# The last block of w2 in two transfers, of 119 rows and of 9 rows

## The chip, the cores and the metric

The kernel runs on one core of one Trainium2 chip. The metric is the device time of one execution in microseconds (us), taken as the median of several executions. The engines are named as in the profile: PE is TensorE, DVE is VectorE, ACT is ScalarE, POOL is GpSimd, SP is SyncE. SP issues nearly all transfers here; "SPq" in the profile is SP's issuing of them.

## What is computed

One decode step of a transformer layer: attention against a cache of 4,096 keys, and then a feed-forward block with the mish activation. Both have a layer norm ahead of them and a residual sum behind. In the reference, cut to what matters:

```python
# A: B=4, Sq=1, D=640, H=32, Sk=4096, Dh=128 (all bf16)
def A(x, k_cache, v_cache, wq, wo):
    q = (x @ wq).reshape(B, Sq, H, Dh).transpose(0, 2, 1, 3)
    scores = einsum("bhqd,bhkd->bhqk", q, k_cache) * Dh ** -0.5
    o = einsum("bhqk,bhkd->bhqd", softmax(scores), v_cache)
    return o.transpose(0, 2, 1, 3).reshape(B, Sq, H * Dh) @ wo

# B: F=1728
def Bff(x, w1, b1, w2):
    h = einsum("bsd,df->bsf", x, w1) + b1
    sp = log1p(exp(-abs(h))) + where(h > 0, h, 0)
    return einsum("bsf,fd->bsd", h * tanh(sp), w2)

h  = x + A(layernorm(x), k_cache, v_cache, wq, wo)
out = h + Bff(layernorm(h), w1, b1, w2)
```

The two caches are 268 MB together; w2 is a matrix of 1,728 rows of 640 numbers, 1,280 B a row.

## The kernel before

The cache is worked through in 16 units, each of eight heads of one batch element. A unit has 8 MB of K and 8 MB of V. Three large buffers of SBUF (`slot`) take turns: while one unit's K is multiplied by the query on DVE (line 614) and summed on PE with an identity matrix (line 626), the next V and K are on their way. The softmax goes over DVE, PE and ACT (lines 663 to 717), the product with V over PE (line 736).

The order of all work is written out by hand. `Program.add` records each operation with the names that it reads and writes; `Program.plan` works out which operation has to wait for which, and `Program.emit` writes the instructions engine by engine, in the order of recording. A transfer raises a semaphore by 16 when it has landed. Where two transfers are given the same semaphore, the counts add up, and who needs both waits once, for the sum.

SP's transfers stand in one queue in the order of recording. Behind the last part of V come, all through the helper `load` (its transfer is line 854): four transfers of wo, five of w1, the 64 remaining rows of w2 (line 873), and then w2 in pieces that get smaller towards the end. The pieces are given by `W2P = (0, 6, 10, 12, C2)` with C2 = 13: blocks 0 to 5, 6 to 9, 10 and 11, and block 12 alone. A block is 128 rows, one row for each partition of SBUF. In the first three pieces a partition takes pairs of neighbouring rows, so each run in memory is 2,560 B; block 12 is odd and has runs of one row, 1,280 B. It is the last transfer into the core.

What reads them stands at the end of the program. Line 941 projects the attention's output by wo; line 901 (`tt`, the helper for sums and products on DVE) adds the residual; lines 978 to 1030 are the second layer norm, with the matmuls by w1 (line 1003) between them; lines 1034 to 1062 the activation. Then PE multiplies by w2 (line 1070): first the remaining 64 rows, then piece by piece, each piece after a wait for its own transfer, named `("w2", k0)`. Five matmuls belong to a block. The sum of all is added to the residual on DVE (line 901), turned by one matmul (line 1087), copied (line 1094), and stored by SP (line 1095) as 20 rows of 256 B.

Of the kernel before, what the change touches and what calls it, by code (L numbers as in the profile page):

```python
# [223 lines left out]
def kernel(  # L224
# [15 lines left out]
    B, Sq, D = A_x.shape  # L240
# [49 lines left out]
    S_BANK, TR, QQ, OB, OT = [("bank", i) for i in range(4)], *[("bank", i) for i in range(4, 8)]  # L290
# [45 lines left out]
    def cells(i, lo=0, hi=SLOT):  # L336

        return [("slot", i, p, k) for p in range(lo // PART, -(-hi // PART)) for k in range(NQ)]
# [470 lines left out]
    def slot_of(u):  # L809
        return 1 if u == 0 else 2 * u % NS  # L810
# [21 lines left out]
    i1, i2, i3 = slot_of(NU - 1), slot_of(NU - 2), slot_of(NU - 3)  # L832
# [7 lines left out]
    w2_sb = wend2[:, 0 : C2 * D].rearrange("p (k n) -> p k n", k=C2)  # L840
    w2r_sb = wend2[:, C2 * D : nw2]
    C2E = C2 - C2 % 2
    w2_view = B_w2[0 : C2E * 128, :].rearrange("(m p k) n -> p m (k n)", p=128, k=2)

    def load(out_ap, in_ap, i, lo, hi, name, sem=None):


        ops = {}
        for cell in cells(i, lo, hi):
            for d in P.readers.get(cell, {}).values():  # L850
                ops[d.nth] = d
        P.add(
            "SP",
            lambda: nc.sync.dma_start(out=out_ap, in_=in_ap),  # L854
            w=[name],
            sem=sem or "_".join(map(str, name)),
            after=ops.values(),
        )
# [18 lines left out]
    for k0, k1 in zip(W2P, W2P[1:]):  # L877
        if k0 < C2E:
            assert k0 % 2 == k1 % 2 == 0
            to = wend2[:, k0 * D : k1 * D].rearrange("p (m n) -> p m n", n=2 * D)  # L880
            of = w2_view[:, k0 // 2 : k1 // 2]
        else:
            to, of = w2_sb[:, k0, :], B_w2[k0 * 128 : k1 * 128, :]
        load(to, of, i2, k0 * D, k1 * D, ("w2", k0))

    at = [nw2]

    def scratch(n, dt=FP32):
        a = at[0]
        w = n * (2 if dt == FP32 else 1)  # L890
        w += w % 2
        at[0] = a + w
        ap = wend2[:, a : a + w]
        return ap.bitcast(FP32)[:, 0:n] if dt == FP32 else ap[:, 0:n]

    def do(eng, emit, r=(), w=()):

        return P.add(eng, emit, r=r, w=w, after=[last_pv])
# [167 lines left out]
    def w2_products(blocks):  # L1066
        for c in blocks:
            w2 = w2_sb[:, c, :] if c < C2 else w2r_sb
            for dc in range(DC):
                ins = nc.tensor.matmul(  # L1070
                    y2T[:, dc, :],
                    lhsT=w2[:, dc * 128 : (dc + 1) * 128],
                    rhs=act_t[:, c, :],
                    start=(c == C2 and dc == 0),
                    stop=(c == C2 - 1 and dc == DC - 1),
                )
        return ins

    do("PE", lambda: w2_products([C2]), ["w2r", "act"], [S_BANK[1]])
    for k0, k1 in zip(W2P, W2P[1:]):  # L1080
        do("PE", lambda b=range(k0, k1): w2_products(b), [("w2", k0), "act"], [S_BANK[1]])
    oT = scratch(N * DC, BF16).rearrange("p (n c) -> p n c", n=N)
    tt(oT.rearrange("p n c -> p c n"), hT, y2T, ALU.add, ["hT", S_BANK[1]], ["oT"])
    o_ps = tr_bank[0 : N * DC, 0:128]
# [45 lines left out]
```

## Time and profile before

| | us |
|---|---|
| median of 3 runs | 667.02 |
| lowest and highest of them | 666.62, 667.08 |
| the profiled execution, its own time | 667.18 |
| its span, first to last instruction | 665.4 |
| busy: PE, DVE, ACT | 378.6, 353.6, 88.5 |
| traffic | 283.52 MB, 426 GB/s in the mean |

The transfers of the end, as the profile lists them by line, form and size, with the median from issue to landing:

| transfer | count | KB each | us to landing |
|---|---|---|---|
| wo | 4 | 1280 | 33.2 |
| w1 | 5 | 432 | 29.7 |
| w2, the remaining 64 rows | 1 | 80 | 20.7 |
| w2, blocks 0 to 5 | 1 | 960 | 20.3 |
| w2, blocks 6 to 9 | 1 | 640 | 19.2 |
| w2, blocks 10 and 11 | 1 | 320 | 13.4 |
| w2, block 12 | 1 | 160 | 12.0 |

A view of the profile counts time from the start of the span. In the chain of waits a line has its start, its length, and the engine and line that the time belongs to. In the DMA view "GB/s" is a row of 40 numbers, one for each fortieth of the window, and "packets" counts the pieces that the 16 DMA engines moved: a piece is one run of a transfer (here a row of w2, or a pair of rows), or a record of 4 B with which an engine reports that its share of a transfer is done.

### The profile page before, as it was taken

What the parts mean: (1) busy time and instruction counts of PE and PEld (TensorE: products, weight loads), DVE (VectorE), ACT (ScalarE), POOL (GpSimd) and SP (SyncE); (2) the same over time, 40 slices, a digit from 0 to 9 for tenths busy, and PEclk for the clock granted to TensorE, in tenths of its full rate; (3) what the DMA queues carried; (4) which work ended last, traced back from release to release, by engine and by line L of the source; (5) the groups of instructions that cost most, each with busy time, mean ns of one, the idle gap of its engine ahead of it and who ended that gap; (6) DMA issues with size and microseconds to landing.
All of it is one profiled execution on the core that took longest, in us unless ns stands there. A gap on an engine that the chain in (4) does not pass through costs nothing.

```text
span 665.4 us, 6915 instructions
## 1 busy us (share of the span) xinstructions
PE 378.6 (57%) x2804; PEld 173.4 (26%) x2804; DVE 353.6 (53%) x315; ACT 88.5 (13%) x316; POOL 2.4 (0%) x12
## 2 busy tenths in 40 slices
PE   0354778375482837558283755828375582827764
PEld 0221333132230313223031322303132230313343
DVE  2075869083573809357380845738084573818501
ACT  0102020202002020200202020020202002020211
POOL 1000000000000000000000000000000000000000
PEclk9999799788596978869697796969779695977965
DMA  9999999999999999999999999999999999999996
GB/s 379 438 441 438 437 415 418 438 437 430 441 437 433 433 418 437 437 429 441 433 437 433 418 437 437 429 441 429 441 433 418 437 437 429 437 433 418 420 415 247
DMA packets 7571, 283.52 MB, mean 426 GB/s; under 512 B 835, under 2 KB 1031, under 8 KB 2440
## 3 DMA queue, kind: packets, MB, share of 16 engines
q1 hardware_dynamic: 7550, 283.35, 99.0%
q8 instruction: 8, 0.13, 0.1%
q14 instruction: 3, 0.02, 0.0%
q10 hardware_dynamic: 10, 0.01, 0.0%
HBM read 283.35 MB, written 0.01 MB: 426 GB/s over the span
## 4 chain that ended last, share of the span: by engine, by line
DMA 43%; DVE 25%; PE 21%; another core or an unknown queue 6%; issue 2%; SPq 1%; ACT 1%; DVEq 0%; ACTq 0%
DMA slot<-in_A_k_cache_dram 41%; DVE slot L614 21%; PE bank L626 13%; PE bank L736 6%; DVE s_sb L601 3%; DMA slot<-in_B_w_dram 2%; SPq L854 1%; ACT e L711 1%; PE bank L694 0%; DVE slot L901 0%; PE bank L769 0%; DVE mx L681 0%; DVE rl L788 0%; PE bank L672 0%
## 5 line engine op out<-in xcount | busy, mean ns | idle before, releaser
L626 PE MATMUL bank<-slot,ident 128*128 128x512 bf16 x1024 | 272.6, 421 | 245.8 <-DVE slot L614 245.8
L614 DVE TENSOR_TENSOR slot<-slot,qb 128x4096 bf16<-128x4096 bf16 x128 | 288.3, 2284 | 156.1 <-DMA slot<-in_A_k_cache_dram 151.6
L626 PEld LDWEIGHTS bank<-slot,ident 128*128 128x128 bf16 x1024 | 101.0, 106 | 402.6 <-DVE slot L614 278.2
L601 DVE TENSOR_REDUCE s_sb<-bank 128x64 f32<-128x512 f32 x64 | 44.0, 688 | 57.3 <-PE bank L626 57.3
L711 ACT ACTIVATE e<-s_sb,nb 128x256 bf16<-128x256 f32 x128 | 63.1, 494 | 46.6 <-DVE nb L703 46.6
L736 PE MATMUL bank<-slot,e 128*32 128x512 bf16 x1024 | 60.9, 392 | 0.0
L581 ACT CAST qb<-bank 128x128 bf16<-128x128 f32 x17 | 4.5, 266 | 307.7 <-PE bank L572 307.7
L736 PEld LDWEIGHTS bank<-slot,e 128*32 128x32 bf16 x1024 | 26.2, 99 | 33.2 <-issue 9.0
L756 ACT COPY o_sb<-bank 128x512 f32<-128x512 f32 x16 | 9.4, 586 | 180.3 <-PE bank L736 180.3
L681 DVE TENSOR_REDUCE mx<-bank 1x8 f32<-1x128 f32 x16 | 4.5, 278 | 39.9 <-PE bank L672 39.9
L711 ACT ACTIVATION_READ_ACCUMULATOR e<-s_sb,nb 128x1 f32 x128 | 23.9, 186 | 0.0
L769 PE MATMUL bank<-sel,o_sb 128*128 128x8 f32 x136 | 17.6, 256 | 0.0
L769 PEld LDWEIGHTS bank<-sel,o_sb 128*128 128x128 f32 x136 | 16.6, 192 | 0.0
L521 PE MATMUL bank<-xT,slot 128*128 128x4 bf16 x160 | 4.4, 168 | 10.7 <-DMA slot<-in_A_wq_dram 10.7
L694 PE MATMUL bank<-mx,nscale 1*128 1x8 f32 x32 | 6.1, 262 | 5.9 <-DVE mx L681 5.9
L788 DVE RECIPROCAL rl<-bank 128x8 f32<-128x8 f32 x17 | 3.4, 201 | 9.1 <-PE bank L769 9.1
L555 DVE COPY b1T<-bank 128x14 f32<-128x14 f32 x1 | 0.2, 173 | 14.0 <-PE bank L545 14.0
L694 PEld LDWEIGHTS bank<-mx,nscale 1*128 1x128 f32 x32 | 4.7, 182 | 10.6 <-DVE mx L681 10.6
L941 PE MATMUL bank<-slot,slot 128*128 128x4 bf16 x160 | 4.9, 166 | 4.4 <-DMA slot<-in_A_wo_dram 4.4
L767 PEld LDWEIGHTS bank<-rs,ones_f 128*128 128x128 f32 x34 | 6.3, 190 | 3.4 <-ACT o_sb L756 1.2
L521 PEld LDWEIGHTS bank<-xT,slot 128*128 128x128 bf16 x160 | 4.3, 104 | 10.8 <-DMA slot<-in_A_wq_dram 10.8
L663 DVE TENSOR_REDUCE pm<-s_sb 128x1 f32<-128x256 f32 x16 | 6.7, 420 | 0.5
(74 smaller groups left out, 70.5 us busy)
## 6 DMA issues: line engine op xcount, KB each, us to landing
slot<-in_A_v_cache_dram SPq DMA_DIRECT2D x4, 2048.0 KB, 42.8
slot<-in_A_wq_dram SPq DMA_DIRECT2D x1, 5120.0 KB, 15.2
slot<-in_A_wo_dram SPq DMA_DIRECT2D x4, 1280.0 KB, 33.2
slot<-in_B_w_dram SPq DMA_DIRECT2D x5, 432.0 KB, 29.7
slot<-in_B_w_dram SPq DMA_DIRECT2D x1, 960.0 KB, 20.3
slot<-in_B_w_dram SPq DMA_DIRECT2D x1, 640.0 KB, 19.2
slot<-in_B_w_dram SPq DMA_DIRECT2D x1, 320.0 KB, 13.4
slot<-in_A_k_cache_dram SPq DMA_DIRECT2D x16, 49.9
```

The source lines that it names most:

```text
L521: ins = nc.tensor.matmul(qT_ps[:, :, h], lhsT=wq_sb[:, c, h * Dh : (h + 1) * Dh], rhs=xT[:, c, :], start=(c == 0), stop=(c == DC - 1),)
L601: lambda: nc.vector.tensor_reduce(out=s_sb[:, part * RP : (part + 1) * RP], in_=s_bank[part][:, :].rearrange("p (r w) -> p r w", w=W), axi ...
L614: return nc.vector.tensor_tensor(out=kt, in0=kt, in1=qbs[u % NS][:, k * DQ : (k + 1) * DQ] .unsqueeze(1) .to_broadcast([128, RP, DQ]), op= ...
L626: ins = nc.tensor.matmul(s_bank[part][:, :].rearrange("p (r w) -> p r w", w=W), lhsT=ident[:, :], rhs=kt[:, :, d : d + W], start=(d == 0), ...
L663: lambda: nc.vector.tensor_reduce(out=pm[:, :], in_=s_sb[:, :], axis=AX.X, op=ALU.max),
L694: lambda: nc.tensor.matmul(nb_ps, lhsT=nscale[:, :], rhs=mx[:, :], start=True, stop=True),
L711: ins = nc.scalar.activation(out=e2[:, :, h, :], in_=s_sb[:, :].rearrange("p (g r) -> p g r", r=RQ), func=ACT.Exp, bias=nb[:, h : h + 1], ...
L736: ins = nc.tensor.matmul(o_bank[t : t + G * RQ, :], lhsT=e2[:, g, :, :], rhs=vt[:, g * RQ : (g + 1) * RQ, :], start=(g < CT), stop=(g >= N ...
L756: lambda: nc.scalar.copy(out=o_sb[:, :], in_=o_bank[:, :]),
L767: nc.tensor.matmul(l_ps, lhsT=ones_f[:, :], rhs=rss[u % NS][:, :], start=True, stop=True)
L769: ins = nc.tensor.matmul(o_ps, lhsT=o_sb[:, r * Dh : (r + 1) * Dh], rhs=sel[:, r, :], start=(r == 0), stop=(r == RQ - 1),)
L854: lambda: nc.sync.dma_start(out=out_ap, in_=in_ap),
```

## The change

Block 12 of w2 comes by two transfers: its first 119 rows, and behind them its last 9 rows. Both are issued by `load` at line 854, one after the other, and raise the same semaphore; the matmuls of block 12 wait for the sum of both. What is read, where it is put and what is computed from it stay the same.

```diff
         if k0 < C2E:
             assert k0 % 2 == k1 % 2 == 0
             to = wend2[:, k0 * D : k1 * D].rearrange("p (m n) -> p m n", n=2 * D)
             of = w2_view[:, k0 // 2 : k1 // 2]
+            load(to, of, i2, k0 * D, k1 * D, ("w2", k0))
         else:
-            to, of = w2_sb[:, k0, :], B_w2[k0 * 128 : k1 * 128, :]
-        load(to, of, i2, k0 * D, k1 * D, ("w2", k0))
+
+            for part, p in enumerate((slice(0, 119), slice(119, 128))):
+                load(
+                    w2_sb[p, k0, :],
+                    B_w2[k0 * 128 + p.start : k0 * 128 + p.stop, :],
+                    i2,
+                    k0 * D,
+                    k1 * D,
+                    ("w2", k0, part),
+                    f"w2_{k0}",
+                )
...
     for k0, k1 in zip(W2P, W2P[1:]):
-        do("PE", lambda b=range(k0, k1): w2_products(b), [("w2", k0), "act"], [S_BANK[1]])
+        names = [("w2", k0)] if k0 < C2E else [("w2", k0, part) for part in range(2)]
+        do("PE", lambda b=range(k0, k1): w2_products(b), [*names, "act"], [S_BANK[1]])
```

## The prediction

> **What bounds the kernel now.** I read the page first: the chain that ended last and the DMA row over the span.
>
> ```profile
> DMA  9999999999999999999999999999999999999996
> ...
> DMA 43%; DVE 25%; PE 21%; another core or an unknown queue 6%; issue 2%; SPq 1%; ACT 1%; DVEq 0%; ACTq 0%
> ```
>
> The 16 DMA engines are busy from end to end; only the last of 40 slices (16.6 us each) shows a 6. The kernel is a stream of 283 MB, and the change touches its last 160 KB, so only the tail counts. I therefore read the chain in order of time over the last 36 us, and SP's timeline beside it:
>
> ```profile
> 640.88 6.68 SPq L854
> 647.57 0.04 issue
> 647.61 13.37 DMA slot<-in_B_w_dram
> 660.98 0.05 issue
> 661.02 0.72 PE bank L1070 x15
> 661.74 0.02 issue
> 661.77 0.23 DVE slot L901
> ```
> ```profile
> 647.61 1.78 SPq L854 DMA_DIRECT2D slot<-in_B_w_dram  x1
> 649.43 0.89 SPq L854 DMA_DIRECT2D slot<-in_B_w_dram  x1
> ```
>
> The first of the two issues is blocks 10 and 11 of w2 (call it piece 10), the second is block 12 (piece 12). Piece 10 lands at 660.98, and its ten matmuls start at 661.02. Piece 12 is the transfer of 160 KB in the list of issues, 12.0 us from issue to landing, so it lands at 649.43 + 12.0 = 661.43; the timeline has the first of its five matmuls there too. After these come only line 901's sum, one matmul, one copy and the store. So two landings, 0.4 us apart, end the kernel.
>
> How does the last one come about? The DMA view cut to two short windows shows it (bytes of 40 slices as GB/s; 75 ns a slice in the first, 15 ns in the second):
>
> ```profile
> core 0 of [0], span 665.4 us
> GB/s 341 341 376 376 358 393 410 393 324 341 307 273 273 307 290 273 307 273 256 171 256 239 171 171 171 239 188 154 103 154 68 68 51 34 34 17 34 17 17 0
> ```
> ```profile
> GB/s 171 0 86 0 0 85 0 86 0 0 85 0 0 0 85 0 0 85 0 0 0 85 0 0 85 0 0 0 85 0 0 85 0 0 0 0 0 0 0 0
> DMA packets 15, 0.02 MB, mean 26 GB/s; under 512 B 4, under 2 KB 14, under 8 KB 15
> ```
>
> The first (658.0 to 661.0) sinks from 393 to 17 GB/s in steps: the engines do not run dry together, they drop out over some 1.7 us. In the second (660.4 to 661.0), 85 GB/s in 15 ns is 1,280 B, one row of w2. From slice 15 on there is one row at slices 15, 18, 22, 25, 29 and 32: five intervals in 17 slices of 15 ns, 51 ns a row, a single engine at its own pace. So a laggard ends the stream: its eight rows of piece 12 (128 rows over 16 engines) take 0.41 us, which is the 0.4 us between the two landings. From its last row (about 660.9) to the matmul is another 0.5 us, the completion.
>
> **The change, part by part.**
>
> *The spread of the rows.* How many engines take a transfer can be read off its completion records (4 B each). Two views show it: the page's row of ScalarE's queue, and the DMA view of the last 2.8 us, which holds only the store.
>
> ```profile
> q10 hardware_dynamic: 10, 0.01, 0.0%
> ```
> ```profile
> DMA packets 30, 0.01 MB, mean 2 GB/s; under 512 B 30, under 2 KB 30, under 8 KB 30
> ```
>
> Queue 10 carries x (4 rows) and b1 (1 row): 5 rows and therefore 5 completions, 4 and 1 engines. The store has 20 rows of 256 B in 30 packets: 10 completions, 10 engines, two rows each. 4, 1 and 10 are the largest counts up to 16 that divide 4, 1 and 20. If this goes on, 119 = 7 x 17 rows go to 7 engines, 17 rows each, and 9 rows to 9 engines, one each. Before, each engine had 8 rows. That is my reading; what 119 rows really do, no row shows, so I bound it:
>
> - One engine takes pieces of both: 18 rows, 10 more than before, 10 x 51 ns = +0.51 us if it is the laggard. Nothing hides this, since the matmuls, line 901's sum and the store all queue behind that landing.
> - The laggard gets none or one of the rows. Then its last landing is piece 10's, which the change cannot bring forward: it was issued earlier and keeps its rows. The ten matmuls from 661.02 are issued some 29 ns apart (the timeline gives 0.43 us for the ten with 0.166 us for one: 0.26 over 9), so the last five can start at 661.31 instead of 661.43: -0.12 us at the most.
>
> ```profile
> 661.02 0.43 PE L1070 MATMUL bank<-slot 128*128 128x4 bf16 x10 [0.15 <-DMA slot<-in_B_w_dram]
> ```
>
> Between these ends: seven engines are lengthened, so the laggard is among them with 7/16. But it isn't alone: an engine that used to finish up to 0.5 us ahead of it, and now gets ten rows more, ends behind the old end. Between 660.25 and 660.55 the first window has 68, 68, 51 and 34 GB/s, 55 in the mean, against 25 GB/s for one engine (1,280 B in 51 ns): two or so were still at work. That none of 2.2 is among the seven has a chance of (9/16)^2.2 = 0.28. So in about seven cases of ten the end moves later by something up to 0.51 us; I take **+0.3 us** and keep -0.12 and +0.51.
>
> The Trainium skill, "DMA: Bandwidth & Descriptors", section "Why a DMA increments its semaphore by 16 and not by 1", gives the rule behind these counts: the largest number up to 16 that divides the slowest dimension, and the lowest-numbered engines. The counts of this trace agree (4, 1, 10); that both pieces start at the same engine, no row here shows. By it seven engines have 18 rows, two have one and seven none, so the sum keeps its ends.
>
> *SP.* One more issue by line 854. It issues in order and blocks while its queue is full: its issues took from 0.33 us (wo) to 6.68 us (the piece of 960 KB). For the new one I take 0.89, the row of piece 12 itself. It lies beside the backlog: the last issue ended at 650.32 and the engines were still busy beyond 658, 8 us of cover. Even 6.68 us would issue the 9 rows before 658. Without any cover it would cost its 0.89 us. What SP does next is the store, waiting for DVE until 662.66, so nothing else is behind it. Price 0.
>
> *PE.* Both transfers raise one semaphore, so the wait ahead of the five matmuls asks for 32 in place of 16: the number of waits and matmuls stays. Queued behind it: those five, line 901's sum, the store; all are in the end already counted. Price 0.
>
> **Sum.** 0 + 0 + 0.3 on the profiled execution of 667.18 us (span 665.4, 1.78 around it). The median of the runs is 667.02, 0.16 less; on it: **667.3 us**. What a measurement can tell from no change is 0.2%, 1.33 us, so this is within it.
>
> **Rivals.**
>
> 1. *The laggard is relieved.* All 18-row engines end ahead of the laggard's piece 10, and the last wait falls on 661.02: -0.12, 666.9 us. For it: most engines are done well before 660.4. Against: seven of 16 are lengthened, and some two are near the end. Chance 0.20.
> 2. *One engine takes the 119 rows* (slower). If counts such as 7 aren't used, all 119 rows run behind each other: with one of the 9, 120 x 51 ns = 6.1 us from where this engine begins. Engines begin piece 12 between about 658.5 (where the rate starts to sink) and 660.5, so its last row comes at 664.6 to 666.6 instead of 660.9: +3.7 to +5.7, about 671.7 us. It decides as soon as the rows on one engine exceed what the laggard leaves, some 8 to 47 rows. For it: no transfer of this trace has an odd count of rows above 1. Against: ten engines for 20 rows shows that counts need not be powers of two. Chance 0.10.
> 3. *The change doesn't do what it says:* 119 rows spread over 16 engines, eight on most, and the nine one each: one row more on some, +0.05, 667.1 us. Against it speaks the store, whose 20 rows didn't go to 16 engines. Chance 0.05.
> 4. *The added issue comes late.* Two issues at 6.68 us behind 649.39 end at 662.75; the 9 rows then land 0.5 us later, at 663.3 instead of 661.43: +1.9, 668.9 us. Only a stall as with the 24-descriptor issue could do this, and the queue is shorter here. Chance 0.03.
>
> A rule of the Trainium skill speaks against the change: same page, "Rules for kernel authors", on two transfers to disjoint partition halves, "Don't bother — they serialize". By it splitting brings nothing and the time would be the 667.0 of before; no run here shows two halves side by side.
>
> **How the numbers follow.** Forecast 0.60 (its own range 666.8 to 667.8: 0 to +0.51 on 667.02, and 0.25 on either side, as the three runs spread over 0.46), rivals 0.20, 0.10, 0.05, 0.03, anything else 0.02. Within 0.2% are the forecast and rivals 1 and 3, 0.85, less 0.03 for shifts the rows don't show: 0.82. Slower: rivals 2 and 4 and a little of the rest, 0.14. Faster by 1.33 us has no mechanism, since piece 10's landing stays: 0.04. The range 666.6 to 668.2 takes in the forecast and rivals 1 and 3, and leaves out 2 and 4.
>
> **What would show it.** In the DMA view of the last microseconds: the tail of single rows at 51 ns, 18 long or gone; and the packets of SP's queue, 7,550 before: the same number again if block 12 still has 16 completions (7 + 9), which confirms the two counts; 6 fewer for 1 + 9, 9 more for 16 + 9. In the chain: the last five matmuls at 661.3 to 661.9. In SP's timeline: an added issue of about a microsecond, ended before 658. The prediction is wrong if the last five matmuls start beyond 662.5, or if piece 10's landing moves from 661.0 by more than 0.5 us.

## The result, and the profile after

The changed kernel takes 667.84 us in the median of 22 executions, the kernel before 666.83 us in as many beside it. The ratio is 1.0013, with a 95% interval of 1.0007 to 1.0019: slower by 0.5 to 1.3 us. That is less than the 0.2% named in the prediction, but it is clear of zero.

The profiled execution took 667.50 us, its span is 665.7. First its page, two lines: the span, and SP's queue with packets, MB and share.

```profile
span 665.7 us, 6916 instructions
...
q1 hardware_dynamic: 7550, 283.35, 98.9%
```

The same line of the kernel before:

```profile
q1 hardware_dynamic: 7550, 283.35, 99.0%
```

One instruction more (the issue), and the same number of packets. So block 12 has 16 completions once more, though it now comes in two parts; a completion is one of the records of 4 B with which an engine reports that its share is done. Now the end of the chain of waits in the changed kernel (start, length, what the time belongs to):

```profile
640.43 6.69 SPq L854
...
647.16 1.78 SPq L854
...
648.98 0.75 SPq L854
649.73 0.05 issue
649.78 11.96 DMA slot<-in_B_w_dram
661.74 0.05 issue
661.78 0.31 PE bank L1080 x5
```

The chain used to go through piece 10 and one block of 15 matmuls. Now it goes through SP's last issue, that of the 9 rows at 649.78, and lands on the last five matmuls alone. PE's timeline shows the same from its side:

```profile
660.99 0.43 PE L1080 MATMUL bank<-slot 128*128 128x4 bf16 x10 [0.45 <-DMA slot<-in_B_w_dram]
661.78 0.30 PE L1080 MATMUL bank<-slot 128*128 128x4 bf16 x5 [0.36 <-DMA slot<-in_B_w_dram]
```

Piece 10 comes when it did (660.99, before 661.02). The five start at 661.78, before at 661.43, and PE now stands idle for 0.36 us ahead of them. All that follows is moved by the same 0.35 us. SP's added issue was over at 651.4:

```profile
649.78 1.65 SPq L854 DMA_DIRECT2D slot<-in_B_w_dram  x1
```

The DMA view of the changed kernel from 660.2 to 661.2 (25 ns a slice, 51 GB/s is one row of 1,280 B):

```profile
GB/s 0 51 51 102 51 51 51 51 51 51 102 0 51 51 51 51 51 51 0 102 0 102 0 51 51 51 51 51 0 0 51 0 51 0 0 0 0 0 0 0
```

Where one engine stood alone with its rows before, two to three now share the end, and the last row is moved at 661.0 (33rd slice). From there it takes 0.77 us until the five matmuls start. Before, it was 0.56 us from the last row at 660.87 to 661.43. So two things are late: the rows, and what follows them.

The packed trace, from which the views are made, has each packet with its start and duration. It shows what these rows are: after 660.35, three engines end one after the other, each with its last rows of the long piece, a completion, one row of the short piece and a second completion (660.51, 660.92 and 661.07). The packets of the last engine can be followed back from end to start: its 18 rows begin at 659.97 and take 1.10 us, 61 ns a row. The eight rows of the laggard before took 0.41 us, 52 ns a row.

The rows are thus not only more on these engines but also slower. In both traces of the kernel before, a row of block 12 takes 55 ns in the mean and 60 at most (the next one starts some 3 ns before the end); in the two traces of the changed kernel the mean is 71 and 66 ns. Why is not shown. It is not the uneven count alone: the splits into 112 and 16 and into 64 and 64 rows below have 63 and 61 ns.

The difference of the two profiles (0.32 us in their own times) is less than that of the medians (1.0 us), since the profiled execution of before took 667.18, above its kernel's median of 666.83, and that of after 667.50, below its median of 667.84. The experiments bring a second profile of before.

### The profile page after: what moved, and what is told of

The parts are those of the page before. It is cut to its first block, busy times and chain, and to the rows that moved or that the text cites. A ratio compares the mean times of both kernels' runs of the same rounds, so it can differ in the third digit from the quotient of the medians.

```text
span 665.7 us, 6916 instructions
## 1 busy us (share of the span) xinstructions
PE 378.4 (57%) x2804; PEld 174.1 (26%) x2804; DVE 353.6 (53%) x315; ACT 88.5 (13%) x316; POOL 2.4 (0%) x12
## 3 DMA queue, kind: packets, MB, share of 16 engines
q1 hardware_dynamic: 7550, 283.35, 98.9%
## 4 chain that ended last, share of the span: by engine, by line
DMA 50%; DVE 22%; PE 17%; another core or an unknown queue 7%; issue 2%; SPq 2%; DVEq 0%
DMA slot<-in_A_k_cache_dram 40%; DVE slot L614 19%; PE bank L626 12%; DMA slot<-in_A_v_cache_dram 7%; PE bank L736 5%; DVE s_sb L601 2%; DMA slot<-in_B_w_dram 2%; SPq L854 2%; PE bank L694 0%; SPq L350 0%; DVE rl L788 0%; DVE mx L681 0%; DVE otn L795 0%; PE bank L672 0%
## 5 line engine op out<-in xcount | busy, mean ns | idle before, releaser
L672 PE MATMUL bank<-ident_f,pm 128*1 128x128 f32 x32 | 6.1, 273 | 1.2 <-DVE pm L663 1.2
```

## The experiments

Two theories. **R**: the ten more rows on the engines that carry both pieces. **S**: a second transfer costs by itself. All edits but `r_before` start from the changed kernel; the number of executions of each is 8 to 12, except where given, and the kernel before ran beside them (medians 667.19, 666.97 and 667.04 us in the three sets).

| run | pieces | rows on the fullest engine | median us | ratio | 95% interval |
|---|---|---|---|---|---|
| r_before | 128 | 8 | 666.82 | 1.0002 | 0.9993 to 1.0011 |
| e1_112_16 | 112, 16 | 8 | 667.21 | 0.9999 | 0.9991 to 1.0008 |
| e12_64_64 | 64, 64 | 8 | 667.25 | 0.9999 | 0.9988 to 1.0009 |
| e7_120_8 | 120, 8 | 9 | 667.23 | 1.0003 | 0.9994 to 1.0012 |
| e3_119_only | 119 | 17 | 667.43 | 1.0000 | 0.9991 to 1.0010 |
| e2_9_first | 9, 119 | 18 | 667.60 | 1.0009 | 1.0000 to 1.0018 |
| r_after | 119, 9 | 18 | 667.63 | 1.0015 | 1.0006 to 1.0024 |
| e8_two_sems | 119, 9 | 18 | 667.87 | 1.0015 | 1.0003 to 1.0026 |
| e11_116_12 | 116, 12 | 30 | 667.44 | 1.0008 | 0.9995 to 1.0022 |
| e10_122_6 | 122, 6 | 62 | 668.62 | 1.0020 | 1.0008 to 1.0032 |
| e4_127_1 (2 executions) | 127, 1 | 128 | 671.72 | 1.0062 | 1.0043 to 1.0081 |
| e9_8x16 | 16, eight times | 8 | 668.52 | 1.0021 | 1.0011 to 1.0031 |

**A balanced split.**

```diff
-            for part, p in enumerate((slice(0, 119), slice(119, 128))):
+            for part, p in enumerate((slice(0, 112), slice(112, 128))):
```

> Block 12 again by two transfers, but of 112 and 16 rows: both counts divide by 16, so each engine has 7 + 1 = 8 rows as before. Theory R (ten more rows on the engines that carry both pieces make the delay of 0.87 us): no change, ratio 0.9995 to 1.0005, the last rows of single engines eight long. Theory S (a second transfer costs by itself, through its issue or a second completion right behind the first): +0.2 us to +0.9 us, ratio 1.0003 to 1.0013, and the five last matmuls start 0.7 us behind the last row instead of 0.5.

No loss that can be measured, as R wants; the interval leaves room for up to 0.08%. Its trace has a little of S. The first line is SP's queue on its page; the next fence is its DMA view from 660 to 661 in 25 ns slices, and the last its chain:

```profile
q1 hardware_dynamic: 7566, 283.35, 99.0%
```
```profile
GB/s 51 102 256 103 154 102 154 256 51 154 154 102 205 154 0 103 103 103 51 0 103 0 51 0 51 0 0 51 0 51 0 51 0 0 0 0 0 0 0 0
```
```profile
661.48 0.31 PE bank L1080 x5
```

16 packets more than before: 32 completions, so both pieces use all 16 engines. The last row is moved in the 32nd slice, at 660.785, and the matmuls start 0.69 us behind it, not 0.56.

**The other order.**

```diff
-            for part, p in enumerate((slice(0, 119), slice(119, 128))):
+            for part, p in enumerate((slice(119, 128), slice(0, 119))):
```

> The same two transfers in the other order, the 9 rows first. Rows per engine as in the changed kernel. R: the same delay as the changed kernel, ratio 1.0007 to 1.0019, since 18 rows stand on seven engines in either order. S in the form that the short piece's completion, close behind another on the same engine, comes late: most of it goes, as 17 rows (0.9 us) now lie between the two completions; the step from the last row to the matmul is 0.5 us again, ratio 1.0000 to 1.0008.

1.0009, between no loss and that of the changed kernel. Its DMA view from 660.2 to 661.2 and a line of its chain:

```profile
GB/s 52 52 102 0 154 0 51 102 0 51 51 51 102 0 51 51 0 102 0 51 51 51 51 0 102 0 102 0 102 0 51 0 0 51 0 0 0 0 0 0
```
```profile
661.66 0.31 PE bank L1080 x5
```

The last row is moved at 661.03 (34th slice) and the matmuls start at 661.66: 0.63 us, so most of the late start has gone with the order, while the rows are as late as in the changed kernel. The trace fits R for the rows and S for the 0.14 us that this order saves; the intervals of the two orders overlap, so the time alone doesn't tell them apart.

**The long piece alone.**

```diff
-            for part, p in enumerate((slice(0, 119), slice(119, 128))):
+            for part, p in enumerate((slice(0, 119),)):
...
-        names = [("w2", k0)] if k0 < C2E else [("w2", k0, part) for part in range(2)]
+        names = [("w2", k0)] if k0 < C2E else [("w2", k0, 0)]
```

> Only the transfer of 119 rows is issued; the last 9 rows of block 12 are left out, and the five matmuls use what stands in those partitions. R: 17 rows instead of 8 on seven engines, nine tenths of the delay stays, ratio 1.0006 to 1.0017. S: one issue and one completion per engine as before, so the ratio is 0.9995 to 1.0005. In the trace R wants 7 completions for block 12: 119 rows + 7 records, SP's queue 7,532 packets; 119 rows on one engine would be 7,526 and on 16 engines 7,541.

This kernel leaves out nine rows of w2. The count came as 7 completions (119 + 7 packets where block 12 had 128 + 16, 18 fewer than 7,550). The line is of its page:

```profile
q1 hardware_dynamic: 7532, 283.34, 99.0%
```

The ratio of 1.0000 is what S expected and lies below R's range of 1.0006 to 1.0017. Its interval reaches to 1.0010, which takes in S and a part of R, so the time is inconclusive; its median is 0.24 us above the kernel before beside it, and 0.2 to 0.4 us below the changed kernel in the other sets. From the last row to the matmuls it is 0.61 us.

**One engine for everything.**

```diff
-            for part, p in enumerate((slice(0, 119), slice(119, 128))):
+            for part, p in enumerate((slice(0, 127), slice(127, 128))):
```

> Pieces of 127 and 1 rows. 127 is prime. If the number of engines is the largest count up to 16 that divides the rows, 127 rows go to one engine, and if the lowest engines are taken first, the one row follows on the same: 128 rows of 51 ns in a line, 6.5 us from where this engine begins (658 to 660.5), so the last row at 664.5 to 667, +3.6 to +6 us, ratio 1.005 to 1.009; 2 completions, SP's queue 7,536 packets. If the rows are spread unevenly over 16 engines (7,550 packets or more): ratio 0.999 to 1.001. Theory S alone: +0.2 to +0.9 us.

The median is 4.5 us above the kernel before, inside what the rule of the counts gives. Page, DMA view from 661.5 to 665, and chain:

```profile
q1 hardware_dynamic: 7536, 283.35, 98.3%
```
```profile
GB/s 29 29 15 29 15 29 15 29 29 15 29 15 29 29 15 29 15 29 29 15 29 15 29 15 29 29 15 29 15 29 29 15 29 15 29 15 29 29 15 29
DMA packets 64, 0.08 MB, mean 23 GB/s; under 512 B 0, under 2 KB 64, under 8 KB 64
```
```profile
649.38 16.73 DMA slot<-in_B_w_dram
666.11 0.05 issue
666.16 0.31 PE bank L1080 x5
```

Two completions: one engine for each piece. A single engine works through the window, 64 rows in 3.5 us, 55 ns a row. The trace has the 128 rows one behind the other, from 658.44 to 665.49, so the one row followed on the same engine: both pieces start at the same engine. This engine begins block 12 at 658.44; the first profile of before still had engines at work until 660.93.

**The two kernels again.**

> The changed kernel once more, for a second profile and a second interval. R: ratio 1.0005 to 1.002 again; the five last matmuls start 0.6 to 0.75 us behind the last row. S expects the same; this run says how far one profile stands for all.

1.0015, the same finding. Its profile fell on an execution 1.5 us above its median, in which piece 10 came late too and the last five matmuls followed the ten at once, so their start says nothing of the step behind the last row. The semaphore does. The packed trace has the time of each raise of a semaphore by a DMA engine, and the last raise for block 12 comes 0.67 us behind the last completion, in this profile and in the first of the changed kernel. In the two profiles of the kernel before it is 0.46 and 0.47 us.

> The kernel before against itself, for a second profile. Ratio 0.9990 to 1.0010; the last row about 0.5 us ahead of the last five matmuls; the last piece of the engines' work is again one engine's eight rows, or, if the laggard of the first profile was chance, several engines end within 0.2 us of each other.

This profile of the kernel before (666.44 us, the lowest of its set) shows what the first did not. Two DMA windows, from 658 to 661 (75 ns a slice) and from 659.2 to 660.2 (25 ns), and a line of the chain:

```profile
GB/s 393 410 376 410 307 393 410 358 341 342 290 307 427 273 324 239 205 256 205 188 171 171 171 188 222 154 120 120 0 0 0 0 0 0 0 0 0 0 0 0
```
```profile
GB/s 256 256 103 358 205 205 102 307 205 205 102 256 205 154 154 154 205 154 154 103 256 154 256 154 256 154 256 154 154 154 154 154 51 205 51 103 0 0 0 0
```
```profile
660.23 0.74 PE bank L1070 x15
```

There is no laggard. Six to eight engines (154 to 205 GB/s at 25 each) work until 660.0 and end together at 660.15, 0.78 us earlier than the one laggard of the first profile. The matmuls of line 1070 follow: the five of block 12 start at 660.66, again 0.56 behind the last row (660.10). So the laggard does not stand at the end of every execution, and in this one many engines do.

**Nearly balanced.**

```diff
-            for part, p in enumerate((slice(0, 119), slice(119, 128))):
+            for part, p in enumerate((slice(0, 120), slice(120, 128))):
```

> Pieces of 120 and 8 rows. 120 is divided by 15, 8 by 8: eight rows on fifteen engines, one more on eight of them, none on the sixteenth. R: one row more (0.05 us), ratio 0.9995 to 1.0006; SP's queue has 7,557 packets (15 + 8 completions). S: +0.1 to +0.2 us of a second completion, in the trace 0.6 to 0.75 us from the last row to the matmuls.

7,557 packets, 15 + 8 completions. The ratio of 1.0003 fits both theories. The five matmuls followed the ten at once, so their start doesn't tell the step. In the packed trace the engine that ends last has a single completion, and its raise follows in 0.46 us, as in the kernel before.

**A semaphore for each piece.**

```diff
-                    f"w2_{k0}",
+                    f"w2_{k0}_{part}",
```

> The changed kernel with a semaphore of its own for each of the two pieces, and so two waits ahead of the last five matmuls. R: as the changed kernel, ratio 1.0005 to 1.002. S, if two counts into one semaphore make the completion late: 0.5 us from the last row's completion record to the matmuls, as before the change; if it is two completions close together on one engine: 0.6 to 0.75 us again.

As slow as the changed kernel, and the matmuls start 0.86 us behind the last row. The last raise comes 0.67 us behind the last completion, as in the changed kernel, so the shared semaphore isn't the cause of its lateness; the rest of the 0.86 lies between the raise and the matmuls, which now wait twice. The two semaphores also show the counts apart: from 659 on, the one of the 119 rows is raised 7 times and that of the 9 rows 9 times.

**Eight pieces.**

```diff
-            for part, p in enumerate((slice(0, 119), slice(119, 128))):
+            for part, p in enumerate(slice(i, i + 16) for i in range(0, 128, 16)):
...
-        names = [("w2", k0)] if k0 < C2E else [("w2", k0, part) for part in range(2)]
+        names = [("w2", k0)] if k0 < C2E else [("w2", k0, part) for part in range(8)]
```

> Block 12 by eight transfers of 16 rows: one row of each on every engine, so eight rows an engine as before, with eight completions in place of one (SP's queue 7,550 + 112 = 7,662 packets). It multiplies by seven what a second balanced transfer costs. R: no row more, ratio 0.9995 to 1.0006. S with the price read from the 112 and 16 rows in the trace (0.13 us more from the last row to the matmuls): if the price comes once for the last completion, +0.1 to +0.3 us, ratio 1.0002 to 1.0006; if every completion adds it, +0.9 us and more, ratio 1.0012 to 1.0020.

Every completion adds to the delay. The page, the DMA view from 661.4 to 662.4 (25 ns a slice), and the chain:

```profile
q1 hardware_dynamic: 7662, 283.35, 98.8%
```
```profile
GB/s 0 0 51 0 51 0 51 0 51 0 0 51 0 51 0 51 0 0 51 0 0 0 0 0 0 0 0 0 0 0 0 0 0 0 0 0 0 0 0 0
```
```profile
653.98 9.48 DMA slot<-in_B_w_dram
663.46 0.05 issue
663.51 0.31 PE bank L1080 x5
```

Eight rows an engine, the last moved at 661.85, and then nothing moves for 1.66 us before the matmuls start: 1.1 us more than the 0.56 of one piece, 0.16 us for each of seven more completions. SP is no part of it; the chain has its last issue at 653.98.

The packed trace shows how this comes about. The last engine's eight completions are 58 ns apart, from 661.50 to 661.91. The last five raises of the semaphore come at 662.72, 662.91, 663.09, 663.28 and 663.46: 185 ns apart. In this trace the raises of one engine thus follow each other more slowly than its rows, and what comes faster has to wait. Seven times 185 less 58 ns is 0.9 us; the completion of piece 10, 57 ns ahead of the first on the same engine, adds 0.1. That is the 1.1 us but for 0.1.

The median is 1.5 us above that of before; 0.4 us of it this step doesn't explain.

**More rows on fewer engines.**

```diff
-            for part, p in enumerate((slice(0, 119), slice(119, 128))):
+            for part, p in enumerate((slice(0, 122), slice(122, 128))):
```

> Pieces of 122 (2 x 61) and 6 rows: two engines, 61 rows each, and one more: 62 rows, 54 more than before. R, with 55 ns a row (the mean over the 128 rows in line) and those engines beginning when engine 0 did with 127 and 1 rows (658.4): last row at 658.4 + 62 x 0.055 = 661.8, matmuls 0.6 behind it at 662.4 instead of 661.4 or 660.7: +1.0 to +1.7 us, ratio 1.0014 to 1.0026; if they begin as late as the last engines (660): +3 us, 1.0045. 8 completions (2 + 6), 7,542 packets. S alone: as the other splits, 1.0003 to 1.0006.

```diff
-            for part, p in enumerate((slice(0, 119), slice(119, 128))):
+            for part, p in enumerate((slice(0, 116), slice(116, 128))):
```

> Pieces of 116 (4 x 29) and 12 rows: four engines with 29 and one more, 30 rows, 22 more than before; 16 completions (4 + 12), 7,550 packets. R: between 658.4 + 1.65 = 660.1 (no loss by the rows) and 660 + 1.65 = 661.7, i.e. 0 to +1.2 us, ratio 1.0003 to 1.0020, more than with 119 and 9 only if the four engines are as late as the seven were. S alone: 1.0003 to 1.0006.

Chain lines of the first and of the second:

```profile
662.80 0.30 PE bank L1080 x5
```
```profile
661.55 0.31 PE bank L1080 x5
```

7,542 and 7,550 packets: 2 + 6 and 4 + 12 completions. 54 rows more on two engines cost 1.3 us by the ratio (0.5 to 2.1), about one and a half times what ten more rows on seven engines cost, and 22 more on four engines less than the ten on seven (1.0008, unclear). So it isn't the number of rows alone: the fullest engine counts only from where it begins. Reckoned back from the last rows at 55 ns, an estimate, the last to end of the two engines began at about 658.7 and that of the four at 659.2; the last to end of the seven in the changed kernel began at 659.97. The engines of these splits were done early with what came before, and had room.

**Two halves.**

```diff
-            for part, p in enumerate((slice(0, 119), slice(119, 128))):
+            for part, p in enumerate((slice(0, 64), slice(64, 128))):
```

> Two transfers of 64 rows, four rows of each on every engine: a second balanced split beside 112 and 16. R: ratio 0.9995 to 1.0005. S: ratio 1.0002 to 1.0006; in the trace, four rows (0.2 us) lie between the two completions of an engine, so the step from the last row to the matmuls should be nearer to 0.5 us than with one row between them.

0.9999, no loss measured. Its DMA view from 660 to 661:

```profile
GB/s 205 102 358 51 154 51 205 51 0 51 0 102 0 51 0 51 0 51 0 0 0 51 0 0 51 0 0 0 51 0 0 51 0 0 0 0 0 0 0 0
```

The last row is moved at 660.78 (32nd slice), and 0.63 us later the matmuls start, as with the 9 rows first. Four rows take some 0.21 us, more than the 185 ns between two raises; with them between the two completions of an engine the second is hardly late.

The step behind the last row, by the completions of the engine that ends last. The first number is from the start of the last row to the first of the five matmuls, the second from the last completion to the last raise of the semaphore. Where the matmuls followed the ten before them at once, the first is left out.

| completions of the last engine | run | row to matmul, us | completion to raise, us |
|---|---|---|---|
| one | before, `r_before` | 0.56, 0.56 | 0.46, 0.47 |
| one | 120 and 8; 119 alone | -, 0.61 | 0.46, 0.51 |
| two, with four or more rows between | 64 and 64; 9 first | 0.63, 0.63 | 0.53, 0.52 |
| two, one row apart | 112 and 16; 122 and 6; 127 and 1; 116 and 12 | 0.69, 0.71, 0.72, 0.72 | 0.60, 0.61, 0.62, 0.62 |
| two, one row apart | changed kernel, `r_after` | 0.77, - | 0.67, 0.67 |
| two, one row apart, two semaphores | `e8_two_sems` | 0.86 | 0.67 |
| eight, one row apart | eight times 16 | 1.66 | 1.56 |

## Why the prediction was right, and where it was off

The measured 667.84 us lies inside the range of 666.6 to 668.2, but in its upper part, and 0.04 above the forecast's own range. The direction and the mechanism of the rows were right; the size was not. The forecast was +0.3 us and the measured change 0.87 us (0.5 to 1.3), so that the time still fell inside is owed to the width of the range. In parts:

- **Seven engines for 119 rows, nine for 9, the same first engine:** shown. The packets give 7, 16 (7 + 9) and 2 completions for 119, for 119 and 9, and for 127 and 1; the raises of the two semaphores give 7 and 9 apart; the 128 rows in a line show the shared engine.
- **The ten more rows, taken at +0.3 us:** the mechanism held, the term was too small. It was weighed as if one laggard and a second engine stood at the end, as in the profile of before. In the execution of `r_before` six to eight did. If any engine is as likely as another to end late, the chance that none of them is among the seven is (9/16)^7, 2%, so nearly the whole of ten rows counts. That chance is an estimate, and the early starts of the two and of the four engines speak against its condition. The rows were also reckoned at 51 ns each; on the last engine of the changed kernel a row took 61. There 18 rows took 1.10 us, where eight took 0.41: 0.69 us more, if the engine would have been last before too.
- **PE's wait at price 0:** the wait is one, as said, but a second completion close behind the first on the same engine makes it end later, by 0.2 us in both profiles of the changed kernel (0.67 us from the last completion to the last raise, against 0.46 and 0.47). This term was missing. Both together are 0.9 us, against 0.87 us measured (0.5 to 1.3). That they agree so well is partly luck, since the first term is taken from two single engines. How the time divides between them is read from traces; the intervals of e1, e3 and e12 alone are too wide to show it.
- **SP's issue at price 0:** right, though it took 1.65 us and not the 0.89 assumed. It ended at 651.4, and even eight issues, with the last at 653.98, weren't what the matmuls waited for.
- **Rival 1, the laggard relieved:** in the profile after, the last three engines to end are ones with both pieces, so it didn't come about.
- **Rival 2, one engine:** not with 119 rows; with 127 it came about, at 4.5 us against the 3.7 to 5.7 worked out for it.
- **Rivals 3 and 4:** refuted by the 7 completions and by SP's timeline.

The rule of the Trainium skill, "DMA: Bandwidth & Descriptors", section "Why a DMA increments its semaphore by 16 and not by 1", agrees with every count here, and with the shared first engine. What the same page says of two halves ("Rules for kernel authors") agrees with 64 and 64: no gain (0.9999).

No version beat the kernel before.

## What to carry to other kernels

The number of rows of a transfer sets how many engines carry it, so a split into 119 and 9 puts 18 rows on some engines and none on others; cut in multiples of 16, or not at all. Where a transfer ends the kernel, the time is set by the engine that finishes last, and its start as well as its rows counts: look at more than one profile before one laggard is taken for a rule. Several small transfers right behind each other at the end pay for every completion, unless each leaves an engine rows enough between two of them.

## What was not expected

Completions of one engine that are a row apart (58 ns) queue up: their raises of the semaphore come 185 ns apart, eight of them end 1.1 us later than one with no row moving in that time, and two semaphores in place of one don't help. The rows themselves became slower with the split, 55 ns before and 66 to 71 after; this stays unexplained. And the engines don't run dry in a fixed picture: the same kernel ended once with one engine alone for 0.4 us and once with six to eight together, 0.78 us earlier.
